# A fused attention, gate and projection kernel: a new written-out table of order, engines and PSUM banks

## The chip, the cores and the metric

The kernel runs on one core of one Trainium2 chip. The metric is device time in microseconds (us): the time of one execution of the whole program, the median of three runs. A profile comes from one further execution, whose own time is given beside it.

## The reference, cut to what matters

There are 8 batches of 8 heads, 576 positions and 64 columns a head. Per head, attention with a cumulative decay:

```
scores = scale * q @ k.T
cum    = cumsum(log(clip(f, 1e-4, 1)))
scores = where(causal, -1e9, scores + cum[:, None] - cum[None, :])
attn   = exp(scores - max);  attn = attn / (sum(attn) + 1e-9)
x      = attn @ v                      # heads side by side: 512 columns
gate   = sigmoid(conv1d over 5 positions of x, one filter a column)
out    = (gate * (x @ w_val)) @ w_out  # both 512 x 512
```

## The kernel before, in words

The work is cut into 32 pairs of heads (four pairs make a batch) and, after every fourth pair, into the two projections of a batch. Every piece of work is a node of a `Plan`: it has a class, the engines that may run it, what it reads and writes, and the PSUM banks that it needs. The classes of one pair, in the order in which they depend on each other:

- loads by DMA, all issued from SyncE: `Xr` (q and k of the pair, two buffers), `vt` (v, two buffers), `dm` (the decay table of one head, broadcast to 128 rows, three buffers) and `dl` (its last part, two halves, two buffers). `dm` and `dl` come from the DRAM table `decd`, which the kernel writes at its start (`tabD`, two transfers; pairs 8 and later read the second).
- `sel`: GpSimd masks `dm` (L314); GpSimd or VectorE adds `tri` to `dl` (L317).
- `TH`, `TL` (from pair 4 on): `Xr` is split into a high part `Xh` (L268) and a low part `Xl` (L394).
- `S` on TensorE in three parts (u = 0, 1, 2; L253), into PSUM; `red` on VectorE (L462) adds the decay and takes the row minimum into `negm`; `SX` on ScalarE (L466) is the exponential into `P` or `Pl`, with its row sum; `rec` (L475, L476) on VectorE takes the reciprocal `rz`.
- `norm`: P times `rz`, on ScalarE (L273), VectorE or GpSimd (L275).
- `PT`: transposes of P on TensorE (L507; L525 and L526 for `Pl`); `PE`: their copies from PSUM to `pt`, on ScalarE or VectorE (L268).
- `PV` on TensorE in two parts (L253), `X`: the copy to `x` (L268), `xh` and `xl`: its high and low part (L268, L576), `conv`: five steps on the gate (the first on any engine, L273 or L275; four on VectorE, L609), `sig`: tanh (L583). For the first two pairs the convolution is a matmul (`CV`) instead.
- per batch `Mv` (x @ w_val, 16 banks of two parts, L253), `H` (times the gate, L641), `hh` and `hl` (high and low, L268, L655), `Mo` (@ w_out, L253), `O` (the copy out, L682 or L684) and `OD` (its DMA).

At the start the two weights come in as 64-bit numbers and are taken apart by VectorE and ScalarE (classes `wv`, `wo`; L698 to L735), in the same first 60 us or so in which the first pairs run. Six blocks of transposes of the identity (`warm`, L368) keep TensorE at work there.

No scheduler runs in the kernel. The order, the engine of each node and its PSUM banks are read from a string, `TABLE`:

```
n, e = DIGITS.index(table[at]) * 64 + DIGITS.index(table[at + 1]), ENGINES[int(table[at + 2])]
...
for k in nd["take"]:
    self.home[k] = range(int(table[at]), int(table[at]) + self.width[k])
    at += 1
...
yield nd["fn"], e
```

Three characters name a node and its engine, and one more each bank that it is the first to touch. Nodes are emitted in the order of the table, so each engine, SyncE's DMA queue among them, runs its own nodes in that order and waits at the first that is not ready. The durations and `mode` numbers that `pe`, `load` and the others are given (`1.55`, `cols=`, `mode=`) were used to find the table; the emitted program does not depend on them.

Of the kernel before, what the change touches and what calls it, by code (L numbers as in the profile page):

```python
# [41 lines left out]
002d001232e02l20W10y32j22o0452m12h23a40X30o40_22x062f20A32k12i12r22t20w30-
12c32g12s10t001122n23c42B31212E11742Q002p22q12v22w13e44n42K012u12y24t43g44r42z12C32D23i41021323m32M022N12O032P22R21422L12A24l41512G12I11621i43z0453p02
3673I005x41a22F33E21912H13u23v13q22S060x33A23n33r12T13s23t12U023C22V13w22J33G22W0633532_021c23x12-
12X12Z11b21d13y23D13o22Y231033J23K13N33B14T061e21g21f23214z25F43P13015D41h21t41k11l23H13F14x34U23_004011n21m23L21o136014V13U2450023311p23Q23711q21r24p
44714A0345649163014613R14v45z41s21E43M24F24811v15L31y23V001w26423T13X073S34G143054B21z13W16514y38T441001x23Y14C11A24413O21B27D48V45J31C14D24H24K0127F4
7x44214E14P24R24L21D31H23Z034I14J23-138054a008_24Z24X34M14N24Y31G14Q14S14O14c014b14g21J21K14-
24W250152156005714d158023911I25914_254035517M15B45e041L25a005b15121M25321O25K35c015g0255d21P45W0365h15j15k21N15f27L36125X25M001275Z25i27N34e14f27z4343
7O15R24j045Y16215_21R15-17J36015T25S15P25N25U11S25O15Q11U26626f16b11V18N48P47P24h031T24i187065n006c25V27B45l016914k16811-
# [759 lines left out]
```

## Time and profile before

| | |
|---|---|
| median of 3 runs | 541.58 us (541.3 to 542.08) |
| the profiled execution | 540.74 us, span 539.0 us |
| granted TensorE clock | 0.999 of full speed |
| busy: TensorE matmul, VectorE, ScalarE, GpSimd | 515.9, 468.1, 424.5, 241.9 us |
| DMA | 95.44 MB, 52.5% of 16 engines |

The span goes from the first to the last instruction; 1.7 us of the profiled execution lie outside it. PE is TensorE's matmuls, PEld its weight loads, DVE is VectorE, ACT ScalarE, POOL GpSimd, SP SyncE. The end of a matmul is modelled in the profile, so a busy PE can hide a short wait.

### The profile page before, as it was taken

What the parts mean: (1) busy time and instruction counts of PE and PEld (TensorE: products, weight loads), DVE (VectorE), ACT (ScalarE), POOL (GpSimd) and SP (SyncE); (2) the same over time, 40 slices, a digit from 0 to 9 for tenths busy, and PEclk for the clock granted to TensorE, in tenths of its full rate; (3) what the DMA queues carried; (4) which work ended last, traced back from release to release, by engine and by line L of the source; (5) the groups of instructions that cost most, each with busy time, mean ns of one, the idle gap of its engine ahead of it and who ended that gap; (6) DMA issues with size and microseconds to landing.
All of it is one profiled execution on the core that took longest, in us unless ns stands there. A gap on an engine that the chain in (4) does not pass through costs nothing.

```text
span 539.0 us, 12792 instructions
## 1 busy us (share of the span) xinstructions
PE 515.9 (96%) x4412; PEld 448.6 (83%) x4412; DVE 468.1 (87%) x1288; ACT 424.5 (79%) x1160; POOL 241.9 (45%) x338
## 2 busy tenths in 40 slices
PE   7878999999999999999999999999999999999997
PEld 5556778888888888888889888899898987898995
DVE  7979999899998998989899989988989897877850
ACT  5989999998678788769987989998888867664312
POOL 3523458363443645365525736657353725123210
PEclk9999999999999999999999999999999999999999
DMA  7987685464446558256575547565475432510112
GB/s 264 280 301 244 210 283 175 143 195 175 162 140 202 176 178 277 93 175 231 181 227 179 161 172 245 196 215 201 165 246 169 150 125 105 198 65 1 40 39 99
DMA packets 29905, 95.44 MB, mean 177 GB/s; under 512 B 3920, under 2 KB 3920, under 8 KB 29840
## 3 DMA queue, kind: packets, MB, share of 16 engines
q1 hardware_dynamic: 29840, 94.62, 52.5%
q8 instruction: 35, 0.57, 0.4%
q14 instruction: 30, 0.25, 0.2%
HBM read 84.69 MB, written 9.91 MB: 176 GB/s over the span
## 4 chain that ended last, share of the span: by engine, by line
PE 61%; DVE 19%; ACT 8%; DMA 5%; issue 4%; SPq 1%; POOL 0%; DVEq 0%; ACTq 0%; POOLq 0%
PE banks L253 51%; PE banks L507 8%; DVE banks L462 5%; DVE gate L609 4%; DMA dl<-decd 3%; ACT P L466 3%; PE banks L525 2%; DVE pt L268 1%; DMA out_dram<-ot 1%; ACT pt L268 1%; SPq L280 1%; DVE P L275 1%; DVE Xl L394 1%; DMA Xr<-in_x_dram 1%; DVE negm L462 1%
## 5 line engine op out<-in xcount | busy, mean ns | idle before, releaser
L466 ACT ACTIVATE P<-banks,negm 128x384 f32<-128x384 f32 (+3 forms) x256 | 135.3, 544 | 25.6 <-DVE negm L462 22.4
L462 DVE CUSTOM_DVE_ANT_0 banks<-banks,dm 128x512 f32<-128x512 f32 (+3 forms) x256 | 119.6, 516 | 9.4 <-PE banks L253 4.0
L253 PE MATMUL banks<-xh,wall 128*128 128x288 f32 x512 | 119.0, 305 | 1.5 <-ACT P L466 0.7
L609 DVE SCALAR_TENSOR_TENSOR gate<-x,cw,gate 128x576 f32<-128x576 f32 x120 | 109.0, 913 | 1.2
L268 ACT COPY pt<-banks 128x256 f32<-128x256 f32 (+2 forms) x217 | 90.3, 451 | 21.7 <-PE banks L507 14.6
L253 PE MATMUL banks<-pt,vt 128*64 128x128 f32 (+2 forms) x1408 | 95.7, 290 | 3.9 <-DVE pt L268 3.0
L314 POOL TENSOR_SCALAR_AFFINE_SELECT dm<-dm 128x256 f32<-128x256 f32 x126 | 62.3, 520 | 80.6 <-DMA dm<-decd 57.6
L507 PE MATMUL banks<-ident,P 128*128 128x128 f32 x640 | 93.1, 276 | 4.9 <-ACT P L466 1.7
L253 PEld LDWEIGHTS banks<-pt,vt 128*64 128x64 f32 x1408 | 83.9, 137 | 15.1 <-issue 5.7
L253 PE MATMUL banks<-wall,hh 128*128 128x512 f32 x288 | 93.3, 405 | 1.2 <-ACT P L466 1.2
L253 PEld LDWEIGHTS banks<-xh,wall 128*128 128x128 f32 x512 | 86.1, 188 | 4.8 <-ACT P L466 1.4
L507 PEld LDWEIGHTS banks<-ident,P 128*128 128x128 f32 x640 | 72.8, 140 | 17.1 <-ACT pt L268 2.7
L275 POOL TENSOR_SCALAR P<-P,rz 128x512 f32<-128x512 f32 (+3 forms) x67 | 48.2, 725 | 72.8 <-DVE rz L476 45.1
L253 PE MATMUL banks<-xl,wall 128*128 128x288 f32 x256 | 75.4, 295 | 0.0
L273 ACT ACTIVATE P<-P,rz 128x512 f32<-128x512 f32 (+3 forms) x117 | 65.6, 586 | 3.8 <-DVE rz L476 3.4
L253 PEld LDWEIGHTS banks<-wall,hh 128*128 128x128 f32 x288 | 50.2, 188 | 10.3 <-ACT P L466 1.7
L253 PE MATMUL banks<-Xh 128*128 128x288 f32 (+4 forms) x280 | 57.2, 338 | 1.3 <-DVE h L641 0.6
L253 PE MATMUL banks<-wall,hl 128*128 128x512 f32 x144 | 56.6, 393 | 0.0
L466 ACT ACTIVATION_READ_ACCUMULATOR P<-banks,negm 128x1 f32 x256 | 55.9, 218 | 0.0
L253 PE MATMUL banks<-Xl,Xh 128*128 128x288 f32 (+4 forms) x280 | 53.1, 313 | 0.1
L253 PE MATMUL banks<-Xh,Xl 128*128 128x288 f32 (+4 forms) x280 | 53.1, 313 | 0.0
L253 PEld LDWEIGHTS banks<-xl,wall 128*128 128x128 f32 x256 | 48.2, 188 | 0.2
(109 smaller groups left out, 871.9 us busy)
## 6 DMA issues: line engine op xcount, KB each, us to landing
dm<-decd SPq DMA_DIRECT2D x62, 640.0 KB, 5.2
Xr<-in_x_dram SPq DMA_DIRECT2D x32, 608.0 KB, 5.5
vt<-in_v_dram SPq DMA_DIRECT2D x32, 320.0 KB, 4.5
out_dram<-ot SPq DMA_DIRECT2D x36, 256.0 KB, 3.7
dl<-decd SPq DMA_DIRECT2D x62, 144.0 KB, 4.5
ot<-in_w_val_dram SPq DMA_DIRECT2D x2, 512.0 KB, 5.3
wu<-in_w_val_dram SPq DMA_DIRECT2D x2, 512.0 KB, 8.9
ot<-in_w_out_dram SPq DMA_DIRECT2D x2, 512.0 KB, 5.8
```

The costliest lines, as they stand in the source:

```text
L253: nc.tensor.matmul(out, lhsT=lhsT, rhs=rhs, start=start, stop=stop)
L268: (eng.copy if eng is nc.scalar else eng.tensor_copy)(out=out, in_=in_)
L273: eng.activation(out=out, in_=in_, func=AF.Copy, scale=col)
L275: eng.tensor_scalar(out=out, in0=in_, scalar1=col, scalar2=0.0, op0=ALU.mult, op1=ALU.add)
L280: lambda e: (nc.sync if e == "SP" else nc.scalar).dma_start(out=out, in_=in_), reads, writes, **kw)
L314: nc.gpsimd.affine_select(out=t, in_=t, pattern=[[0, 2], [-1, P]], base=0, channel_multiplier=1, compare_op=ALU.is_ge, fill=-BIG)
L394: eng.tensor_tensor(out=Xl[r][:, a:e], in0=Xr[r][:, a:e], in1=Xh[r][:, a:e].bitcast(F32), op=ALU.subtract)
L462: nc.vector.tensor_tensor_reduce(out=sl, in0=sl, in1=add[:, o:o + ext], op0=ALU.add, op1=ALU.min, scale=-0.125, scalar=3.0e38, accum_out=n ...
L466: nc.scalar.activation(out=dst[:, o:o + ext], in_=bank(key)[:, c0:c0 + ext], func=AF.Exp, bias=negm[r][:, col], scale=-1.0, accum_out=zs[r ...
L507: nc.tensor.transpose(out=bank(key)[:, c:c + P], in_=Pt[m][:, BOFF[b] + P * j:BOFF[b] + P * j + P], identity=ident)
L525: nc.tensor.transpose(out=bank(key)[:, P * j:P * j + P], in_=Pl[r][:, D + P * j:D + P * j + P], identity=ident)
L609: eng.scalar_tensor_tensor(out=gt, in0=src, scalar=wt_, in1=gt, op0=ALU.mult, op1=ALU.add)
```

## The change

The table is another one for the same 2868 entries: all lines of it differ. Every node has the same function, reads and writes, and every matmul, transfer and copy is still there once. What differs is the order on each engine, the banks, and, for classes that more than one engine may run, which engine it is. Counted in the two tables (where the counts differ by more than 2):

| class | before | after |
|---|---|---|
| `norm` on ScalarE, VectorE, GpSimd | 137, 75, 76 | 113, 49, 126 |
| `TH` on ScalarE, VectorE, GpSimd | 24, 14, 18 | 28, 3, 25 |
| `TL` on VectorE, GpSimd | 29, 27 | 25, 31 |
| `PE` copies on ScalarE, VectorE | 217, 103 | 206, 114 |
| `X` on ScalarE, VectorE | 46, 18 | 51, 13 |
| `xh` on ScalarE, VectorE | 23, 9 | 19, 13 |
| `hh` on ScalarE, VectorE | 22, 10 | 17, 15 |
| `hl` on VectorE, GpSimd | 21, 11 | 18, 14 |
| `O` on ScalarE, VectorE | 23, 13 | 27, 9 |
| `sel` on GpSimd, VectorE | 83, 12 | 88, 7 |

The first transfers of SyncE's queue are, before: f, f, conv_w, w_val, vt(1), Xr(0), w_val, vt(0), decd(0), Xr(1), decd(1), dm(2), w_val, dm(0), dm(1), dl(0), dl(1), dl(0), dl(1), Xr(0), w_val, Xr(1). After: f, f, conv_w, w_val, w_val, Xr(0), vt(1), vt(0), decd(0), Xr(1), dl(1), dl(1), dm(2), w_val, dm(0), dl(0), dl(0), Xr(0), dm(1), w_val, dl(1), Xr(1), decd(1).

The other edits change numbers that only served to find the table:

```diff
-0240630040B30930C40E10b20430u000r010N40s000a20c20d10520F20H20I10G20z30e20J20f23k40q010h10K20g20740Y40L20k10l12940i20j20M20P10m42b30Q20S20T10R20U20V20v
...
+0040b20x30930240C40a20E10430520c20y30F20s010H20G20d10e20630t000I10J20f20N40K20Y40g20L20j20M20k20l20740h10i10P10Q20S20R20T10u000U20W10r003k42940m43a42d
...
-        load("load", 1.55, i - (1.0 if i else 9.0), Xr[r], x[i], (), [("Xr", r)], early=i == 0)
+        load("load", 1.95, i - (1.0 if i else 9.0), Xr[r], x[i], (), [("Xr", r)], early=i == 0)
...
-            load("dec", 1.6, p + 0.05 * h, dm[m], decd[2 * i + h:2 * i + h + 1, 0:SW].to_broadcast([P, SW]), dk, [("dm", m)])
+            load("dec", 2.05, p + 0.05 * h, dm[m], decd[2 * i + h:2 * i + h + 1, 0:SW].to_broadcast([P, SW]), dk, [("dm", m)])
...
-        load("tabD", (0.7, 2.0)[n], z - 0.5, decd[r0:r1], st[r0:r1], [*ktab, *kst], [("decd", n)])
+        load("tabD", (0.35, 0.9)[n], z - 0.5, decd[r0:r1], st[r0:r1], [*ktab, *kst], [("decd", n)])
...
-            pe("S", (1.15, 0.905, 0.87)[u] * more * two, p, go, opd + tab,
+            pe("S", ((1.15, 0.902, 0.79), (1.41, 0.97, 1.067))[i < NF][u] * two, p, go, opd + tab,
...
-            pe("PT", 0.109 * nt, p, go, [("ident",), *(("P", m, b) for b in blocks)], [key], cols=256 * nt, mode=0)
+            pe("PT", 0.109 * nt, p, go, [("ident",), *(("P", m, b) for b in blocks)], [key], cols=256 * nt, mode=2)
...
-            load(nm + "D", 1.8, p - 0.5, wu[w], src[c * P:(c + 1) * P].bitcast(I32), (), uk + kl)
+            load(nm + "D", 1.3, p - 0.5, wu[w], src[c * P:(c + 1) * P].bitcast(I32), (), uk + kl)
```

## Rows read from the trace of the kernel before

**Rows 1.** The page: busy time, share of the span and instructions of each engine; then the engines' shares of the chain of work that ended last.

```profile
PE 515.9 (96%) x4412; PEld 448.6 (83%) x4412; DVE 468.1 (87%) x1288; ACT 424.5 (79%) x1160; POOL 241.9 (45%) x338
PE 61%; DVE 19%; ACT 8%; DMA 5%; issue 4%; SPq 1%; POOL 0%; DVEq 0%; ACTq 0%; POOLq 0%
```

**Rows 2.** Busy time of each engine in five stretches: the stretch, its length, then PE, PEld, DVE, ACT and POOL busy us (with instruction counts), the granted clock, the DMA share and GB/s.

```profile
0.00:31.00 31.00, 22.68 (x153) 16.42 (x153) 24.09 (x79) 21.59 (x57) 13.39 (x36) 1.00 0.89 275
31.00:141.00 110.00, 104.04 (x894) 85.76 (x891) 104.32 (x296) 101.26 (x276) 51.88 (x66) 1.00 0.63 211
141.00:475.00 334.00, 328.91 (x2946) 292.38 (x2946) 303.82 (x843) 278.17 (x774) 164.16 (x224) 1.00 0.54 181
475.00:535.00 60.00, 60.00 (x430) 54.04 (x426) 35.90 (x73) 22.89 (x54) 12.48 (x13) 1.00 0.13 46
535.00:539.03 4.03, 0.25 (x2) 0.00 (x0) 0.00 (x0) 0.60 (x1) 0.00 (x0) 0.81 0.35 130
```

**Rows 3.** The timeline at the start: start us, duration us, engine, line, operation, tiles and shapes, count, and in brackets the idle time before it with what ended it.

```profile
3.00 4.53 PE L368 MATMUL banks<-ident 128*128 128x128 f32 x20 [3.00 <-POOL ident L323]
10.23 1.56 PE L253 MATMUL banks<-Xr 64*128 64x512 f32 x8 [0.48 <-DMA Xr<-in_x_dram]
29.07 0.23 DVE L317 TENSOR_TENSOR dl<-dl,tri 128x64 f32<-128x64 f32 x1 [2.75 <-DMA dl<-decd]
29.57 1.64 PE L253 MATMUL banks<-pt,vt 128*64 128x192 f32 x20 [2.63 <-DVE pt L268]
```

**Rows 4.** The chain of work that ended last, in order of time: start us, us, what.

```profile
3.63 6.56 DMA Xr<-in_x_dram
19.30 9.68 DMA dl<-decd
```

**Rows 5.** SyncE's queue at the start: when a transfer was issued, and for how long the queue was at it.

```profile
3.63 0.43 SPq L280 DMA_DIRECT2D Xr<-in_x_dram  x1
12.66 0.33 SPq L280 DMA_DIRECT2D dm<-decd  x1
17.52 2.37 SPq L280 DMA_DIRECT2D dl<-decd  x4
```

**Rows 6.** Transfers in the first 40 us: all of them, then by destination and source the count, KB each and the median us from issue to landing.

```profile
DMA packets 3363, 11.22 MB, mean 281 GB/s; under 512 B 573, under 2 KB 573, under 8 KB 3360
dm<-decd SPq DMA_DIRECT2D x5, 640.0 KB, 7.0
Xr<-in_x_dram SPq DMA_DIRECT2D x4, 608.0 KB, 8.4
wu<-in_w_val_dram SPq DMA_DIRECT2D x2, 512.0 KB, 8.9
vt<-in_v_dram SPq DMA_DIRECT2D x3, 320.0 KB, 6.2
dl<-decd SPq DMA_DIRECT2D x6, 144.0 KB, 8.8
```

**Rows 7.** Groups of instructions by line, engine, operation and shape: count, busy us and mean ns of one, then the idle time before them and what ended it.

```profile
L609 DVE SCALAR_TENSOR_TENSOR gate<-x,cw,gate 128x576 f32<-128x576 f32 x120 | 109.0, 913 | 1.2
L275 POOL TENSOR_SCALAR P<-P,rz 128x512 f32<-128x512 f32 x20 | 16.8, 845 | 19.8 <-DVE rz L476 13.4 <-ACT pt L268 3.6 <-PE banks L253 1.4
L273 ACT ACTIVATE P<-P,rz 128x512 f32<-128x512 f32 x30 | 21.9, 738 | 0.6 <-DVE rz L476 0.5
L275 DVE TENSOR_SCALAR P<-P,rz 128x512 f32<-128x512 f32 x14 | 7.1, 508 | 0.2
L268 POOL CAST Xh<-Xr 128x576 fp32r<-128x576 f32 x12 | 8.2, 686 | 4.9 <-DMA Xr<-in_x_dram 4.9
L268 DVE CAST Xh<-Xr 128x576 fp32r<-128x576 f32 x6 | 3.6, 608 | 0.0
```

**Rows 8.** Single lines: count, then ns of one, shortest/median/longest, first and last start us, shapes.

```profile
L609 DVE SCALAR_TENSOR_TENSOR gate<-x,cw,gate x120: 778/819/1993, 68.3 to 511.1; 128x576 f32<-128x576 f32 x120
L314 POOL TENSOR_SCALAR_AFFINE_SELECT dm<-dm x126: 398/407/1098, 3.2 to 469.9; 128x256 f32<-128x256 f32 x126
L275 DVE TENSOR_SCALAR P<-P,rz x72: 259/410/1581, 17.3 to 474.8; 128x256 f32<-128x256 f32 x22, 128x384 f32<-128x384 f32 x19, 128x128 f32<-128x128 f32 x17, 128x512 f32<-128x512 f32 x14
L275 POOL TENSOR_SCALAR P<-P,rz x67: 364/692/1602, 16.2 to 487.7; 128x512 f32<-128x512 f32 x20, 128x128 f32<-128x128 f32 x20, 128x256 f32<-128x256 f32 x16, 128x384 f32<-128x384 f32 x11
```

**Rows 9.** TensorE alone, around a change from transposes to `PV` and from `PV` to `Mv`, and inside a run of `Mv`.

```profile
502.12 0.38 PE L507 MATMUL banks<-ident,P 128*128 128x128 f32 x2
502.43 2.95 PE L253 MATMUL banks<-pt,vt 128*64 128x192 f32 x44
505.31 0.40 PE L253 MATMUL banks<-xh,wall 128*128 128x288 f32 x1
505.55 0.30 PE L253 MATMUL banks<-xl,wall 128*128 128x288 f32 x1
...
512.95 0.30 PE L253 MATMUL banks<-xh,wall 128*128 128x288 f32 x1
513.08 0.29 PE L253 MATMUL banks<-xl,wall 128*128 128x288 f32 x1
```

**Rows 10.** Who waited for whom, in total: us, times, longest.

```profile
POOL P L275 <- DVE rz L476: 45.1, 16, 6.0
ACT P L466 <- DVE negm L462: 22.4, 25, 2.6
```

More of the change, by code (lines that the diff above doesn't have):

```diff
@@ L40 @@
 TABLE = """
-0240630040B30930C40E10b20430u000r010N40s000a20c20d10520F20H20I10G20z30e20J20f23k40q010h10K20g20740Y40L20k10l12940i20j20M20P10m42b30Q20S20T10R20U20V20v
[L42 to L49, printed above, removed]
@@ new lines @@
+37437607a2aX1e21c407dD3g24dT0542729V1c517728F2dJ02613262br47b1bW2dC3dU2eI4283d-
+2c22c01b707dQ2dR19X1dK2b503dL1fW4dW28G3c31ce02dM2fY4dO2dP17c37e0dY2dZ1bY3b62c12dN1c603b81b_37i06cc079Y2eK49Z2b91dS2bb17f19W27g47j0eW2c71d_1e52cf1cd17n
+019-
+2ha4dX19_2ba2e41e72cg074cj2eU37o0ch2dV17k1ca00ck1e32e93eb3bc2ci28M1fg02fh2bd2gb1cb1be2fi1ef05hi4e62cn07eS37p1g91cl03e81eZ02401cm17q4dA4eT3co2cp2f7063c
+r3eg1ea3e-
+2f22hg4f31e_1gc3ed05f02f42fe2f11fa2ho3a017s07eh00f51ee2ei1cq37l47t07u1el02cA04fb1ec2ej01cB0hr1ek1f82ff1g63cs2cx05cy0bf2f62em1bg1ep023cC2ct2er1cI04fm1f
@@ L370, in tile_decay_attention_gated_mlp @@
         wk = new(("warm", n))
-        pe("warm", 0.436, z, lambda wk=wk: warm(wk), [("ident",)], [wk], cols=1024, mode=0)
+        pe("warm", 0.436, z, lambda wk=wk: warm(wk), [("ident",)], [wk], cols=1024, mode=2)
     def mk_tri():
@@ L526, in gol @@
             nc.tensor.transpose(out=bank(key4)[0:D, 0:P], in_=Pl[r][:, 0:D], identity=ident)
-        pe("PT", 0.48, p, gol, [("ident",), ("Pl", r)], [key, key4], cols=1152, mode=0)
+        pe("PT", 0.545, p, gol, [("ident",), ("Pl", r)], [key, key4], cols=1152, mode=2)
         for h in range(2):
@@ L564, in plan_pv @@
             names = ((1, 2), (3, "l", "l4"))[half]
-            pe("PV", (1.36, 1.515)[half], p, go, [*vk, *(("pt", m, n) for m in ms for n in names), *(("pt0", m) for m in ms)], [key],
+            pe("PV", (1.36, 1.465)[half], p, go, [*vk, *(("pt", m, n) for m in ms for n in names), *(("pt0", m) for m in ms)], [key],
                cols=(6144, 7168)[half], mode=3)
@@ L599, in gocv @@
                         mm(bank(key)[:, 0:e - a], dv[t], xr[:, t + a:t + e], t == 0, t == KC - 1)
-                pe("CV", 2.55, p + 0.1 + 0.02 * half, gocv, [*xk, ("xpad", r), *dk], [key], cols=5760, mode=0)
+                pe("CV", 2.55, p + 0.1 + 0.02 * half, gocv, [*xk, ("xpad", r), *dk], [key], cols=5760, mode=2)
                 act("CE", 0.3, p + 0.1 + 0.02 * half, lambda key=key, a=a, e=e: half_tanh(gt[:, a:e], bank(key)[:, 0:e - a]), [key], [gk])
@@ L636, in plan_moe @@
                     cs = (2 * c2, 2 * c2 + 1)
-                    pe("Mv", 0.8, p + 0.5 * MS * c2, go, [*((x, (G * b + c) % NX) for c in cs for x in ("xh", "xl")),
+                    pe("Mv", 0.79, p + 0.5 * MS * c2, go, [*((x, (G * b + c) % NX) for c in cs for x in ("xh", "xl")),
                                                          *((w, c) for c in cs for w in ("wv", "wvh"))], [key], cols=1728, mode=0)
@@ L674, in plan_moe @@
                 js2 = (2 * half, 2 * half + 1)
-                pe("Mo", 1.37, p + half * MS, go, [*((x, jj, n) for jj in js2 for x in ("hh", "hl") for n in names),
+                pe("Mo", 1.36, p + half * MS, go, [*((x, jj, n) for jj in js2 for x in ("hh", "hl") for n in names),
                                                  *((w, jj) for jj in js2 for w in ("wo", "woh"))], [key], cols=3072, mode=0)
```

137 lines of the change are left out of this document (71 added, 66 removed).

## The prediction

> **What bounds the kernel now.** I began with the page. TensorE's matmuls are busy for 515.9 of 539.0 us and hold 61% of the chain that ended last; VectorE follows with 468.1 us and 19% [rows 1]. The number and the shapes of the matmuls are the same in both tables, so the order can only give back time in which TensorE waits, or what it loses when it changes from one form of matmul to another. Its visible idle time is 23.1 us, and the table of stretches says where it lies [rows 2]: 31.0 - 22.7 = 8.3 us up to 31 us, 110.0 - 104.0 = 6.0 us from 31 to 141 us, 334.0 - 328.9 = 5.1 us from 141 to 475 us, nothing from there to 535 us, and 3.8 us at the end. The granted clock is 1.00 in the four stretches that hold matmul work, so no clock is to be won. The last 3.8 us are the last copy and its transfer, which both tables order alike. Of the first 8.3 us, 3.0 are the wait for the identity, also left as it is [rows 3]. So 8.3 - 3.0 + 6.0 + 5.1 = 16.4 us can be won in what the profile shows. It is a floor: ends of matmuls are modelled, and a short wait disappears in them.
>
> The three stretches have different causes. At the start the largest single wait of TensorE is 2.63 us, before the second half of the first `PV`, for a small VectorE copy [rows 3]. That copy stood behind VectorE's `dl` add, which had waited 2.75 us for a transfer [rows 3]; that transfer was issued at 19.30 us and took 9.68 us [rows 4]. From 31 to 141 us VectorE is busy for 104.3 of 110 us (95%) and ScalarE for 101.3 (92%) [rows 2]: here these two set the pace, since the weights are decoded beside the pairs. From 141 to 475 us they fall to 91% and 83% [rows 2]; what TensorE waits for then is short and comes from single chains.
>
> **The change, part by part.**
>
> *Transfers at the start.* The late `dl` is moved ahead of the second `decd` table, three `dm`, one `w_val` block and the two `dl` of the other buffer. By the sizes [rows 6] that is at least 3 x 640 + 512 + 2 x 144 = 2720 KB, which at the 281 GB/s of the first 40 us [rows 6] is 9.7 us. In the old queue the first `dm` went out at 12.66 us, and the four `dl` began at 17.52 us [rows 5]. The add on `dl(1)` is GpSimd's in the new table, so that VectorE would not stand before it even if it were late. I count the 2.6 us as gone. Against it, `Xr(0)` now has a second `w_val` (512 KB) ahead of it instead of a `vt` (320 KB): 192 KB or 0.7 us later. It was issued at 3.63 us and took 6.56 us [rows 4, 5], and TensorE waited 0.48 us for it [rows 3], so nothing covers the delay at that point. Net 2.6 - 0.7 = 1.9 us. The bounds are 0 (VectorE, freed, runs into the extra decoding below) and 2.6.
>
> *Work moved between engines.* I priced each node by the time from its start to the start of its engine's next node, the lower quartile of its class and size, which leaves queueing and collisions out; the groups of rows show the order of size. A normalisation of 128x512 takes 508 ns on VectorE, 738 on ScalarE and 845 on GpSimd; a cast `TH` of 128x576 takes 608 on VectorE and 686 on GpSimd [rows 7]. By these sums VectorE's work falls from 424 to 412 us, ScalarE's from 399 to 382, and GpSimd's rises from 208 to 251. Where it falls matters more. Along the first 120 us of matmul work, which end at 141 us in the old run, VectorE goes from 121.4 to 114.8 us, ScalarE from 115.5 to 114.6, GpSimd from 55.4 to 75.2. Within it, the first 60 us get 2.5 us heavier on VectorE (61.6 to 64.1) and stay level on ScalarE (59.0 and 59.1); from 60 to 120 VectorE loses 9.1 us (59.8 to 50.7). VectorE is therefore no longer saturated in the second half; in the first it has more to do, which the 2.75 us of waiting removed above pays for. Of the 6.0 us I count 2.5 as won: not all, because ScalarE hardly gets lighter there. Bounds: 0 and 6.0.
>
> *Chains in the middle.* For each of the 595 steps of TensorE I took the latest matmul step on which it depends through other engines, added the row durations of the nodes between, and compared that with the matmul work that the table puts between the two. This says nothing of queues; it counts places where the order leaves little room. Steps with less than 1 us of room fall from 103 to 62: from 14 to 14 in the first 60 us of matmul work, 13 to 10 in the next 60, 66 to 34 from 120 to 440, 10 to 4 behind that. Where the number is halved I take half of the visible 5.1 us, 2.5 us. Bounds: 0, since the new order has places of its own (a `vt` issued 2.2 us of matmul work ahead of its `PV`, where a `vt` of the first 40 us took 6.2 us to land [rows 6]), and 5.1.
>
> *Changes of form.* Three forms follow each other on TensorE: full tiles (`Mv`, `Mo`, `PT`, `S` u = 2), 64 rows (`S` u = 0, 1) and 64 columns (`PV`). After a `PV` the first `Mv` matmul takes 0.24 us to the next start, 505.31 to 505.55, where inside a run it takes 0.13, 512.95 to 513.08 [rows 9]: about 0.1 us a change. The tables have 130 and 127 changes: 0.3 us. Bounds 0.3 and, were every change 0.2 us, 0.6. The Trainium skill (TensorEngine Tiling (Array Packing), Key Properties) says that a change of tiling mode drains TensorE. The rows agree that a change costs something; with three fewer of them the sum stays as it is.
>
> *Nothing else in the diff reaches the chip:* the other numbers were only used to search.
>
> Sum: 1.9 + 2.5 + 2.5 + 0.3 = 7.2 us off the profiled 540.7 us: 533.5 us. The median of the runs lies 0.8 us above the profiled execution, so a median of 533.5 to 534.3; I say 534, and 0.2% (1.1 us) is about what a measurement of this kernel can tell from no change.
>
> **The rivals.**
>
> *The waits form again.* A table fixes who waits for whom; a wait that goes may only move. For it speaks that ScalarE is at 92% from 31 to 141 us and keeps its 114.6 us there, and that VectorE has 2.5 us more in the first 60. If the middle gains nothing and the saturated stretch 0.5, the sum is 1.9 + 0.5 + 0.3 = 2.7 us: 538 to 539 us. Against it: room grew in the middle in nearly half of the tight places.
>
> *GpSimd and VectorE hold each other up; the kernel gets slower.* The trace shows that they do: the convolution steps (L609) take 778 ns at best, 819 in the median, 1993 at worst, with a mean of 913 [rows 7, 8], which is 120 x 0.094 = 11.3 us lost by VectorE on this line alone, and GpSimd's masks go from 398 to 1098 ns [rows 8]. The new table gives GpSimd some 70 more instructions, 50 of them normalisations between `rec` and a transpose, where GpSimd already is idle for 45.1 us before `rz` is there [rows 10] and so starts at once, colliding with whatever VectorE does next. If each held VectorE up for half of a 0.6 us instruction, that is 70 x 0.3 = 21 us against the 12 us taken off it: 9 us more, of which the stretch up to 141 us, which gets 19.8 of the 43 us, has 4. With the 1.9 us of the start that makes 544 us; with late transposes in the middle as well, 548. It decides from about 12 / 0.3 = 40 collisions of 70 on. Against it: at the present rate, 11.3 us for 241.9 us of GpSimd, 43 us more cost L609 2 us. The Trainium skill (SBUF — State Buffer, Who interferes with whom) states the rule behind this: GpSimd and a VectorE instruction with two SBUF inputs, or in a two-port mode, exclude each other for a whole instruction. The spread of L609 agrees; by that rule a normalisation moved to GpSimd saves VectorE less than its length.
>
> *More than the sum.* If both saturated engines let go from 31 to 141 us and the waits hidden in modelled ends go as well, 1.9 + 6.0 + 5.1 + 0.3 = 13.3 us: 527 to 528 us.
>
> *The change does nothing,* because what differs is hidden: excluded by the 2.6 us wait, unless something equal takes its place; that is the first rival at its far end.
>
> **How the numbers follow.** Forecast (530 to 537 us) 0.55; waits form again (537 to 541.5) 0.20, of which 0.06 within 0.2%; slower 0.13, nearly all of it above 543; more than the sum (under 530) 0.10; 0.02 for what I don't see, put at no change. Faster 0.55 + 0.10 + 0.14 = 0.79, within 0.2% 0.08, slower 0.13. The range leaves out the slow case and the far end of the best: 527.5 to 541.5; the forecast's own is 530 to 537.
>
> **What would show it.** Right: no wait of over 1 us before a `PV` in the first 35 us, and no VectorE `dl` add behind a transfer; TensorE's first `S` some 0.7 us later; VectorE under 90% busy in the second half of the stretch up to 141 us, PE idle there about 3.5 us; in the middle about 2.5 us; GpSimd about 290 us busy, L609's mean still near 0.9 us. Wrong: L609's mean above 1.05 us, or transposes (L507) that wait for GpSimd's P; or the 2.6 us found again under another name before 60 us.

## The result, and the profile after

The new table runs in 526.69 us, the median of four runs (525.57 to 527.36); the old one beside it in 541.44 us (538.9 to 542.08). The ratio is 0.9734, with an interval of 0.9698 to 0.977: 14.8 us less. Beside the later runs the old kernel took 539.7 to 540.5 us in the median, so 13 to 15 us is what the change is worth. The forecast was 534.0 us, with a range of 527.5 to 541.5: the direction was right, the gain about twice as large, and the time lies 0.8 us outside the range. The profiled execution took 527.36 us, its span 525.6 us (539.0 before). Line numbers of the new kernel are 3 higher than those of the old (L609 is now L612, L507 is L510, L253 is L256).

The page of the new kernel: busy time, then the engines' shares of the chain that ended last. It answers [rows 1].

```profile
PE 510.6 (97%) x4412; PEld 448.0 (85%) x4412; DVE 450.2 (86%) x1257; ACT 410.1 (78%) x1121; POOL 292.1 (56%) x408
PE 79%; ACT 9%; DVE 5%; DMA 3%; issue 2%; SPq 1%; POOL 0%; DVEq 0%; ACTq 0%
```

VectorE's share of the chain fell from 19% to 5%, TensorE's rose from 61% to 79%. And TensorE is busy for 5.3 us less than before, with the same 4412 matmuls at the same granted clock. Since the ends of matmuls are modelled, that can hardly be quicker arithmetic. It is mostly waiting that the old profile showed as work, as the count from start to start below bears out.

Stretches of the new run; it answers [rows 2] (columns as there), with the second stretch in two halves.

```profile
0.00:31.00 31.00, 24.73 (x162) 17.70 (x163) 25.81 (x82) 22.78 (x59) 14.84 (x40) 1.00 0.80 265
31.00:86.00 55.00, 51.45 (x429) 40.34 (x429) 51.81 (x151) 53.27 (x149) 37.35 (x50) 1.00 0.73 242
86.00:141.00 55.00, 54.36 (x492) 48.92 (x489) 49.67 (x140) 49.67 (x135) 36.01 (x49) 1.00 0.58 192
141.00:475.00 334.00, 333.12 (x3020) 300.16 (x3019) 294.30 (x832) 270.47 (x755) 196.90 (x267) 1.00 0.55 182
521.00:525.60 4.60, 0.89 (x4) 0.38 (x3) 0.00 (x0) 0.60 (x1) 0.00 (x0) 1.00 0.29 110
```

The same two halves of the old run:

```profile
31.00:86.00 55.00, 50.42 (x403) 38.77 (x400) 51.97 (x156) 54.59 (x153) 24.35 (x31) 1.00 0.70 234
86.00:141.00 55.00, 53.62 (x493) 46.98 (x492) 52.34 (x141) 46.67 (x124) 27.53 (x35) 1.00 0.56 189
```

Visible idle time of TensorE is now 6.3 us up to 31 us (8.3 before), 3.6 + 0.6 = 4.2 us up to 141 us (6.0), 0.9 us up to 475 us (5.1) and 3.7 us at the end (3.8): 8.1 us less in all, of 13.4 us by which the span fell. The rest is in the counts. From 141 to 475 us the old run issued 2946 matmuls [rows 2], the new one 3020 in the same 334 us. A busy matmul took 328.91 / 2946 = 111.6 ns there, now 333.12 / 3020 = 110.3 ns. The mix of shapes in the two windows is not quite the same, but 1.3 ns x 3020 = 4 us is most of the 5.3 us that the busy time lost.

The start of the new run (timeline; columns as in [rows 3]):

```profile
10.48 2.07 PE L256 MATMUL banks<-Xr 64*128 64x512 f32 x8
17.59 0.44 PE L510 MATMUL banks<-ident,P 128*128 128x128 f32 x2 [1.17 <-ACT P L276]
26.02 2.94 PE L256 MATMUL banks<-pt,vt 128*64 128x128 f32 x44
```

The whole first `PV` follows without a wait, where 2.63 us stood before its second half [rows 3]. Groups by shape, against [rows 7], and the single line of the convolution, against [rows 8]:

```profile
L612 DVE SCALAR_TENSOR_TENSOR gate<-x,cw,gate 128x576 f32<-128x576 f32 x120 | 104.9, 879 | 1.3
L278 POOL TENSOR_SCALAR P<-P,rz 128x512 f32<-128x512 f32 x27 | 22.1, 819 | 31.8 <-DVE rz L479 23.7 <-ACT gate L586 6.1 <-DVE rz L478 2.1
```

```profile
L612 DVE SCALAR_TENSOR_TENSOR gate<-x,cw,gate x120: 778/819/1744, 67.8 to 503.3; 128x576 f32<-128x576 f32 x120
```

With 50 us more on GpSimd the mean of the convolution step fell from 913 to 879 ns, the longest from 1993 to 1744. So the extra work on GpSimd did not lengthen this step in the new order.

**Waits counted from start to start.** Busy time hides waits, starts don't. For each of TensorE's 595 steps I took the time from its last matmul's start to that of the next step, and, as the time that this transition needs, about the quickest sixth of the same pair of kinds in the old run. The sum of the latter is called matmul work (500.6 us before, 499.1 after); what is above it is waiting: 30.5 us before, 19.0 after. With the first matmul at 2.7 instead of 3.0 us this makes 1.5 + 11.5 + 0.3 = 13.3 of the span's 13.4 us. By place, on the scale of matmul work: up to 25 us 7.7 and 6.6; from 25 to 120 us (141 us of time in the old run) 10.8 and 8.4; from 120 to 440 us 11.5 and 3.7; behind that 0.5 and 0.4. So the middle gave 7.8 us, three times the term in the forecast. The split depends on how the pairs are grouped: grouped by class of step alone, the same starts give 30.9 us before and 18.2 after, 14.6 and 8.5 of them in the middle. Other groupings put the fall in the middle between 6 and 9 us, more than twice the term in each.

### The profile page after: what moved, and what is told of

Its sections match the earlier page's. It is cut to its first block, busy times and chain, and to the rows that moved or that the text cites. A ratio compares the mean times of both kernels' runs of the same rounds, so it can differ in the third digit from the quotient of the medians.

```text
span 525.6 us, 12791 instructions
## 1 busy us (share of the span) xinstructions
PE 510.6 (97%) x4412; PEld 448.0 (85%) x4412; DVE 450.2 (86%) x1257; ACT 410.1 (78%) x1121; POOL 292.1 (56%) x408
## 4 chain that ended last, share of the span: by engine, by line
PE 79%; ACT 9%; DVE 5%; DMA 3%; issue 2%; SPq 1%; POOL 0%; DVEq 0%; ACTq 0%
PE banks L256 64%; PE banks L510 12%; ACT P L469 3%; PE banks L528 2%; DMA Xr<-in_x_dram 2%; DVE banks L465 2%; ACT P L276 1%; ACT pt L271 1%; DMA dm<-decd 1%; SPq L283 1%; DMA Pl<-in_f_dram 1%; PE banks L529 1%; ACT Xh L271 0%; ACT gate L701 0%; ACT x L271 0%
## 5 line engine op out<-in xcount | busy, mean ns | idle before, releaser
L469 ACT ACTIVATE P<-banks,negm 128x128 f32<-128x128 f32 (+3 forms) x256 | 134.2, 535 | 22.0 <-DVE negm L465 20.7
L278 POOL TENSOR_SCALAR P<-P,rz 128x128 f32<-128x128 f32 (+3 forms) x113 | 77.4, 691 | 98.0 <-DVE rz L479 69.4
L465 DVE CUSTOM_DVE_ANT_0 banks<-banks,dm 128x128 f32<-128x128 f32 (+3 forms) x256 | 120.0, 513 | 11.5 <-PE banks L256 4.5
L256 PE MATMUL banks<-xh,wall 128*128 128x288 f32 x512 | 120.2, 306 | 0.0
L612 DVE SCALAR_TENSOR_TENSOR gate<-x,cw,gate 128x576 f32<-128x576 f32 x120 | 104.9, 879 | 1.3
L510 PE MATMUL banks<-ident,P 128*128 128x128 f32 x640 | 99.2, 276 | 4.2 <-ACT P L276 1.2
L271 ACT COPY pt<-banks 128x512 f32<-128x512 f32 (+2 forms) x206 | 84.5, 444 | 22.4 <-PE banks L510 10.7
L256 PE MATMUL banks<-pt,vt 128*64 128x128 f32 (+2 forms) x1408 | 95.6, 290 | 0.3 <-DVE pt L271 0.3
L256 PE MATMUL banks<-wall,hh 128*128 128x512 f32 x288 | 93.3, 405 | 0.0
L256 PEld LDWEIGHTS banks<-pt,vt 128*64 128x64 f32 x1408 | 83.6, 137 | 11.2 <-issue 2.4
L510 PEld LDWEIGHTS banks<-ident,P 128*128 128x128 f32 x640 | 75.4, 140 | 16.5 <-POOL P L278 1.8
L256 PEld LDWEIGHTS banks<-xh,wall 128*128 128x128 f32 x512 | 86.3, 188 | 0.7
L256 PE MATMUL banks<-xl,wall 128*128 128x288 f32 x256 | 75.4, 294 | 0.0
L317 POOL TENSOR_SCALAR_AFFINE_SELECT dm<-dm 128x256 f32<-128x256 f32 x126 | 56.7, 475 | 29.4 <-DMA dm<-decd 21.8
L271 DVE COPY pt<-banks 128x512 f32<-128x512 f32 (+2 forms) x114 | 49.3, 450 | 17.1 <-PE banks L510 10.4
L276 ACT ACTIVATE P<-P,rz 128x256 f32<-128x256 f32 (+3 forms) x100 | 58.2, 597 | 5.9 <-DVE rz L479 5.8
L256 PE MATMUL banks<-Xh 128*128 128x288 f32 (+4 forms) x280 | 57.6, 340 | 0.4 <-ACT P L469 0.4
L256 PEld LDWEIGHTS banks<-wall,hh 128*128 128x128 f32 x288 | 50.2, 189 | 7.7 <-ACT P L469 0.2
L256 PE MATMUL banks<-wall,hl 128*128 128x512 f32 x144 | 56.7, 394 | 0.0
L256 PE MATMUL banks<-Xh,Xl 128*128 128x288 f32 (+4 forms) x280 | 52.9, 313 | 0.0
L256 PE MATMUL banks<-Xl,Xh 128*128 128x288 f32 (+4 forms) x280 | 52.9, 313 | 0.0
```

Source lines behind the costliest of these rows:

```text
L256: nc.tensor.matmul(out, lhsT=lhsT, rhs=rhs, start=start, stop=stop)
L271: (eng.copy if eng is nc.scalar else eng.tensor_copy)(out=out, in_=in_)
L276: eng.activation(out=out, in_=in_, func=AF.Copy, scale=col)
L278: eng.tensor_scalar(out=out, in0=in_, scalar1=col, scalar2=0.0, op0=ALU.mult, op1=ALU.add)
L317: nc.gpsimd.affine_select(out=t, in_=t, pattern=[[0, 2], [-1, P]], base=0, channel_multiplier=1, compare_op=ALU.is_ge, fill=-BIG)
L465: nc.vector.tensor_tensor_reduce(out=sl, in0=sl, in1=add[:, o:o + ext], op0=ALU.add, op1=ALU.min, scale=-0.125, scalar=3.0e38, accum_out=n ...
```

## Experiments

Theory: the new order is fitted to its engines, so that TensorE finds its data in the middle; each stretch earns its part by itself. Rivals: it is less load on VectorE and ScalarE that does it, or the new engines by themselves, or the quicker start. One thing is not separated: the PSUM banks and SyncE's queue went with the order in every run but two on the queue's start, so "order" below means all three together. In kernels with a spliced or exchanged table the lines have other numbers again (L242 is L253, L496 is L507, L306 is L317, L598 is L609 of the old kernel; L610 is L609 where work is cut). All runs in one table, waits by place in matmul work:

| kernel | median us | up to 21.5 | 21.5 to 134.5 | 134.5 to 275 | behind | sum |
|---|---|---|---|---|---|---|
| before | 541.44 | 7.6 | 11.3 | 6.0 | 5.7 | 30.5 |
| after | 526.69 | 6.4 | 8.6 | 1.1 | 2.9 | 19.0 |
| ordB_engA | 599.37 | 6.3 | 20.3 | 30.0 | 31.7 | 88.4 |
| ordA_engB | 595.20 | 8.9 | 23.3 | 25.2 | 30.5 | 87.9 |
| b_norm_A | 552.04 | 6.3 | 12.4 | 12.2 | 12.0 | 42.9 |
| a_norm_B | 563.96 | 10.1 | 19.5 | 7.5 | 17.4 | 54.5 |
| b_dve_short | 533.80 | 5.6 | 10.7 | 3.7 | 3.0 | 22.9 |
| b_act_short | 538.19 | 5.7 | 11.2 | 6.4 | 5.9 | 29.2 |
| b_pool_short | 538.04 | 4.6 | 11.8 | 4.9 | 6.5 | 27.7 |
| b_all_short | 528.85 | 5.0 | 7.3 | 2.4 | 2.7 | 17.5 |
| a_dve_short | 525.22 | 5.7 | 7.2 | 1.4 | 2.1 | 16.4 |
| a_all_short | 522.41 | 5.2 | 5.3 | 1.1 | 2.5 | 14.1 |
| b_dl_early | 539.64 | 5.5 | 11.5 | 6.0 | 6.5 | 29.5 |
| a_xr_first | 526.04 | 5.2 | 8.2 | 1.2 | 3.7 | 18.3 |
| ab_177 | 539.48 | 6.0 | 12.9 | 6.6 | 6.4 | 32.0 |
| ba_177 | 528.20 | 6.8 | 6.5 | 1.1 | 2.8 | 17.2 |
| ab_892 | 536.16 | 6.2 | 10.5 | 6.2 | 6.2 | 29.1 |
| ba_892 | 534.56 | 5.9 | 13.4 | 3.4 | 3.4 | 26.1 |
| ab_1716 | 529.82 | 6.6 | 8.4 | 1.2 | 6.3 | 22.5 |
| ba_1716 | 538.95 | 5.2 | 12.6 | 7.0 | 3.3 | 28.0 |

The old kernel beside these runs took 539.7 to 540.5 us in the median; where a few tenths matter the ratio is given. A row is one profile: before and ba_1716 have the same table up to 275 us of matmul work and yet read 7.6 and 5.2, 11.3 and 12.6, 6.0 and 7.0 us there, so a difference of 1 or 2 us between two cells tells nothing.

### Order or engines

One kernel keeps the old order and banks and takes the new engine of every node, the other does the reverse; 484 of 1036 nodes that have a choice change engine. The edit of the string is written out here in words:

```diff
 entry of the old table, in the old order:
-(node, engine_before[node], banks_before[node])
+(node, engine_after[node], banks_before[node])
 and in the new order:
-(node, engine_after[node], banks_after[node])
+(node, engine_before[node], banks_after[node])
```

> The order and the banks of the kernel before, with every node on the engine that the new table gives it. Theory 1 (the order on TensorE gives the time, by the room that it leaves between dependent steps): this kernel has 111 matmul steps with less than 1 us of room, as the one before (103), so it stays at 539 to 545 us, or gets slower by what badly placed nodes cost. Theory 2 (the relief of VectorE and ScalarE gives the time): VectorE is 12 us and ScalarE 17 us lighter here too, so most of the 14.8 us comes: 528 to 533 us.

> The order and the banks of the new table, with every node on the engine that it had before. Theory 1 (order and room): 63 steps with less than 1 us of room, as the new kernel (62), so most of the gain stays: 527 to 532 us. Theory 2 (relief of VectorE and ScalarE): the load is the old one, 536 to 542 us. Sum of the two: if each gives a part, both crossed kernels lie between 529 and 539 us.

Measured: 599.37 us, ratio 1.1098 (1.1056 to 1.1139), and 595.20 us, 1.1017 (1.0972 to 1.1061). Both theories fell: neither part alone gains anything, each costs: 59 us against the old kernel, 68 us against the new one. In the first, transposes wait for everybody; the second line is the old kernel's:

```profile
L496 PE MATMUL banks<-ident,P 128*128 128x128 f32 x640 | 96.8, 279 | 23.6 <-DVE pt L257 5.8 <-ACT P L455 4.9 <-POOL P L264 4.8
L507 PE MATMUL banks<-ident,P 128*128 128x128 f32 x640 | 93.1, 276 | 4.9 <-ACT P L466 1.7 <-ACT P L273 1.1 <-DVE P L275 0.9
```

23.6 us of idle time stand before this line instead of 4.9. The second also has 63 places with less than 1 us of room by my count, as few as the new kernel (62), and 87.9 us of waits: the count that carried the forecast's middle term does not predict waits once queues are disturbed. An engine runs its nodes in the table's order, so a node on another engine delays all that stands behind it there. Not all of the 87.9 us is waiting for data: in the second kernel the granted clock is 0.97 from 141 to 475 us, where both originals have 1.00, and by that figure some 0.03 x 334 = 10 us (an estimate) are lost to the lower clock:

```profile
141.00:475.00 334.00, 302.63 (x2567) 262.45 (x2565) 275.33 (x735) 247.77 (x680) 153.37 (x206) 0.97 0.49 163
```

The milder exchange, of the 288 normalisations alone (171 change engine):

```diff
 normalisations in the old order:
-(node, engine_before[node], banks_before[node])
+(node, engine_after[node], banks_before[node])
 normalisations in the new order:
-(node, engine_after[node], banks_after[node])
+(node, engine_before[node], banks_after[node])
```

> The old order and banks; only the 288 normalisations run on the engines of the new table (171 change engine, 50 more on GpSimd), all else on the old engines. Theory 1 (only together): in proportion to the full exchange, 58 us for 484 nodes, 20 us: 555 to 565 us. Theory 2 (the normalisations on GpSimd are the gain): 528 to 535 us. Theory 3 (hardly matters): 539 to 543 us. The forecast's slower rival (GpSimd holds VectorE up, 544 to 548 us) would show here as a mean of L609 above 1.05 us.

> The new order and banks; only the 288 normalisations run on the engines that the old table gave them (171 of them change engine, GpSimd goes from 126 back to 76), all else on the new engines. Theory 1 (order and engines of a table only work together, every node on another engine stands in a queue that was not laid out for it): in proportion to the full exchange, 70 us for 484 nodes, 171 nodes cost 25 us: 545 to 556 us. Theory 2 (the normalisations on GpSimd are what the change gains by): their gain alone is lost, some 540 us. Theory 3 (where a normalisation runs hardly matters): 527 to 530 us.

Measured: 552.04 us, ratio 1.0227 (1.0206 to 1.0247), and 563.96 us, 1.0448 (1.0418 to 1.0478). The costs are 12 us and 37 us where proportion gave 20 and 25. Both times lie outside every range that was expected: only together, yes, in proportion, no. The new order depends on where its normalisations run three times as much as the old. The first run also tests the slower rival of the forecast: 50 more normalisations on GpSimd, in an order that was not made for them. The kernel does get slower, but not by a longer convolution step. Its line, that of b_pool_short (next section; GpSimd's normalisations and masks cut), and the transposes of the first run:

```profile
L598 DVE SCALAR_TENSOR_TENSOR gate<-x,cw,gate 128x576 f32<-128x576 f32 x120 | 107.7, 902 | 1.5 <-ACT gate L262 0.3
L610 DVE SCALAR_TENSOR_TENSOR gate<-x,cw,gate 128x576 f32<-128x576 f32 x120 | 102.3, 857 | 1.2
L496 PE MATMUL banks<-ident,P 128*128 128x128 f32 x640 | 95.3, 279 | 12.8 <-DVE P L264 3.7 <-ACT P L455 2.4 <-POOL P L264 2.0
```

The mean is 902 ns against 913 in the old kernel. What grew is the idle time before the transposes, from 4.9 to 12.8 us, waiting for P from all three engines; the kernel lost 12 us. By these rows it is late data in the queues that costs, not two engines that hold each other up. The Trainium skill (SBUF — State Buffer, Who interferes with whom) lets such pairs exclude each other. The spread of single instructions agrees [rows 8], and b_pool_short shows a price: with less work on GpSimd the step takes 857 ns, 6.7 us less on this line than in the old kernel. That more work on GpSimd lengthens the step, no run here shows.

### Load or order

Work of one engine is cut while order and engines stay: convolution steps on 64 of 576 columns and VectorE's normalisations on 16 (VectorE), normalisations on 16 columns (ScalarE), normalisations and masks on 16 (GpSimd), and the three together. The edit for VectorE:

```diff
-                times(eng, sl, sl, rz[r][:, c:c + 1])
+                w = 16 if eng in (nc.vector,) else sl.shape[-1]
+                times(eng, sl[:, 0:w], sl[:, 0:w], rz[r][:, c:c + 1])
...
-                    eng.scalar_tensor_tensor(out=gt, in0=src, scalar=wt_, in1=gt, op0=ALU.mult, op1=ALU.add)
+                    eng.scalar_tensor_tensor(out=gt[:, 0:64], in0=src[:, 0:64], scalar=wt_, in1=gt[:, 0:64], op0=ALU.mult, op1=ALU.add)
```

> The kernel before, with VectorE's work cut: its 120 convolution steps (L609) work on 64 of 576 columns and its normalisations on 16, which takes some 90 us off VectorE and nearly all of its collisions with GpSimd on these lines; the output leaves that work out. If VectorE's pace, its own load and what GpSimd takes from it, is what makes TensorE wait in the old order, most of the 14.8 us comes: 526 to 530 us. If the old order itself leaves too little room, or the other engines are late, it stays above 535 us.

> The kernel before, with ScalarE's 137 normalisations cut to 16 columns, some 45 us off ScalarE; the output leaves that work out. If ScalarE's pace makes TensorE wait (92% busy up to 141 us, 83% behind that): 528 to 534 us. If not: 538 to 541 us.

> The kernel before, with GpSimd's normalisations and masks cut to 16 columns, some 80 us of its 242; the output leaves that work out. If late GpSimd results and its collisions with VectorE are what the old table did not foresee and the new one does: 528 to 534 us. If neither matters: 538 to 541 us.

> The kernel before, with the three cuts together. This is the floor of the old order on TensorE: matmul work, changes of form, transfers and chains that no relief shortens. If the pace of the engines is the whole difference to the new kernel: at or under 526 us. If the old order on TensorE is itself worse: 530 us or more.

Measured in the old order: VectorE 533.80 us, 0.9873 (0.9832 to 0.9914); ScalarE 538.19, 0.9952 (0.9931 to 0.9973); GpSimd 538.04, 0.9951 (0.9928 to 0.9975); all three 528.85, 0.9793 (0.9752 to 0.9833). The first and the last lie between the ranges that were expected. Of the three cuts VectorE's takes most: behind 134.5 us of matmul work 5.0 of 11.7 us of waits. Up to there it takes hardly any, though VectorE falls from 104.3 to 93.8 us of work between 31 and 141 us; TensorE issues as many matmuls in that stretch as in the old kernel, 894 [rows 2]:

```profile
31.00:141.00 110.00, 104.15 (x894) 86.14 (x894) 93.77 (x300) 101.23 (x277) 49.55 (x68) 1.00 0.62 209
```

With all three cut the old order still takes 528.85 us, more than the new order with its full work, 526.69. In the middle the cuts leave VectorE 249 us and ScalarE 254 us of work, where the new table leaves them 294 and 270. So less load alone is not what the change gained by; that it has a part in the gain is not excluded.

> The new table, with VectorE's work cut: the convolution steps (L612) on 64 of 576 columns and VectorE's normalisations on 16 columns, the same cut that took the old table from 540.5 to 533.8 us. Only the amount of work is changed, so the output is not the reference's. Theory 1 (the new order has taken out what TensorE waited for VectorE in the middle, 12.3 us down to 3.7): little is left to take, 1.5 to 3 us, so 523.5 to 525.5 us, with 2.5 us or more of waiting left between 120 and 440 us of matmul work. Theory 2 (VectorE sets the pace of the new table as well, the gain came from somewhere else): as much is taken as from the old one, 6.7 us or more, so 520 us or less.

> The new table, with the work of VectorE, ScalarE and GpSimd cut together as in the old table's run at 528.85 us (convolution steps on 64 columns, normalisations and masks on 16); the output is not the reference's. Theory 1 (the gain of the change lies in an order that fits its engines, so that load matters less in it): the cut takes less than the 12 us that it took from the old table, 4 to 7 us: 520 to 523 us. Theory 2 (the two orders differ only in how much work they put beside TensorE): with the work gone both come out alike, 527 to 529 us, or the cut takes as much as before, 12 us, 515 us.

Measured in the new order: 525.22 us, 0.9726 (0.9706 to 0.9746), and 522.41 us, 0.9671 (0.9651 to 0.9692). The VectorE cut, worth 6.2 us to the old order, is worth 1.5 us here at most (by the ratios, 0.9726 against 0.9734, less than half of that); all three, worth 11.2 us, give 4.3 us. Both times lie in the first theory's ranges. The middle shows it by the count of matmuls in one stretch; before and after have 2946 and 3020 there.

The old order, VectorE cut:

```profile
141.00:475.00 334.00, 332.10 (x2997) 298.52 (x2996) 255.61 (x851) 280.00 (x785) 150.00 (x224) 1.00 0.55 183
```

The old order, all three cut:

```profile
141.00:475.00 334.00, 332.58 (x3008) 299.41 (x3007) 249.02 (x841) 254.20 (x785) 122.72 (x226) 1.00 0.54 181
```

The new order, all three cut:

```profile
141.00:475.00 334.00, 333.23 (x3023) 300.03 (x3023) 243.10 (x825) 248.64 (x751) 135.07 (x268) 1.00 0.56 181
```

The new order with its full work issues 3020 matmuls, with the three cuts 3023: in its middle the work that was cut costs TensorE next to nothing. It is not all of the work, for VectorE and ScalarE are still busy for 243 and 249 of the 334 us. The old order gets from 2946 to 3008 with the same cuts and stays 12 short of the new order with its full work.

### Each stretch by itself

Up to some entries the two tables name nearly the same nodes (3 of 177, 7 of 892 and 5 of 1716 differ). There they can be spliced (the splices at 1716 in the same way).

```diff
-TABLE = before
+TABLE = after[:892] + [e for e in before if e.node not in after[:892]]
 and its mirror image:
-TABLE = after
+TABLE = before[:892] + [e for e in after if e.node not in before[:892]]
```

> New table up to its 892nd entry (134 us of matmul work, some 155 us of time), then the old table's order, engines and banks for all that is left; the first 892 entries of the two tables name the same nodes but for 7. From the starts of the matmuls, the new run reaches this seam 4.6 us ahead of the old one (153.4 against 158.0 us). Theory 1 (each stretch of the new order carries its own part of the gain): the old order behind the seam keeps its own waits, 540.4 - 4.6 = 536 us, 534.5 to 537.5, and the two kernels spliced at this entry add up to the two originals, 540.4 + 526.7 = 1067 us, within 3 us. Theory 2 (a table only works as a whole: what goes before sets how late the queues run in what follows): 3 us or more worse than that, 539 us or more, or all of the gain is here, 530 us or less.

> The mirror image: the old table up to its 892nd entry, then the new table's order, engines and banks for the rest. Theory 1 (each stretch carries its own part): 13.4 - 4.6 = 8.8 us off the old time, 531.6 us, 530 to 533.5. Theory 2 (the middle of the new order is only quick because its start was): 535 us or more.

> New table up to its 1716th entry (275 us of matmul work, some 300 us of time; 5 of 1716 nodes differ), then the old one. By the starts of the matmuls the new run is 9.5 us ahead there (294.7 against 304.2 us). Theory 1 (own part in each stretch): 540.4 - 9.5 = 530.9 us, 529 to 533. Theory 2 (only as a whole): 534 us or more, or the full gain, 527.5 us or less.

> The old table up to its 1716th entry, then the new one. Theory 1 (own part in each stretch): 13.4 - 9.5 = 3.9 us off, 536.5 us, 534.5 to 538. Theory 2: 539.5 us or more, so that the later part gains nothing by itself.

Measured: ab_892 536.16 us, 0.9925 (0.9906 to 0.9944), where 536 was expected; ab_1716 529.82, 0.981 (0.9793 to 0.9828), where 530.9 was; ba_892 534.56, 0.9903 (0.9864 to 0.9941), 3 us more than expected; ba_1716 538.95, 0.9984 (0.9954 to 1.0014), 2.4 us more and between the two theories, with ten runs from 536.1 to 542.8. Of the four, ab_892 and ab_1716 lie in the first theory's ranges, the two others in none. The waits show where: behind the seam ab_892 has 6.2 and 6.2 us, the old order's 6.0 and 5.7; ab_1716 has 8.4 and 1.2 before its seam (the new order's 8.6 and 1.1) and 6.3 behind; ba_1716 has 3.3 behind its seam (the new order's 2.9). ba_892 has 3.4 and 3.4 where the new order has 1.1 and 2.9, and 13.4 in front instead of 11.3. That is the seam: a wait of 1.93 us for a normalisation at 157.6 us, and then a stretch at a lower clock (last section). The pairs of mirror images add up to 1070.7 and 1068.8 us against 1066.4 for the originals (539.7 + 526.7); the first pair misses the 3 us that were allowed by 0.7, and the seam's wait and clock are of that size. So the stretches up to both seams earn their part by themselves, and ba_892, 5.1 us under the old kernel in spite of its seam, shows the same for what lies behind 892. For the last stretch it isn't shown by the time: ba_1716 is 0.7 us under the old kernel, an interval that takes in no change, and only its waits behind the seam, 3.3 against 5.7 us, speak for it.

### The start

The old table with the two late `dl` moved up, the new table with `Xr(0)` ahead of the second `w_val`, and the splice at entry 177:

```diff
 SyncE's queue of the old table:
-decd(0), Xr(1), decd(1), dm(2), w_val, dm(0), dm(1), dl(0), dl(1), dl(0), dl(1), Xr(0), w_val, Xr(1)
+decd(0), Xr(1), dl(1), dl(1), dm(2), w_val, dm(0), dm(1), dl(0), dl(0), Xr(0), w_val, Xr(1), decd(1)
 of the new table:
-conv_w, w_val, w_val, Xr(0), vt(1)
+conv_w, w_val, Xr(0), w_val, vt(1)
 and the splice:
-TABLE = before
+TABLE = after[:177] + [e for e in before if e.node not in after[:177]]
```

> The kernel before, with three entries of SyncE's queue moved at the start: both dl(1) transfers right behind Xr(1), the second decd table behind the second Xr(1). All else as before. If the 2.6 us wait before the second half of the first PV is time of the whole kernel: 539 to 539.5 us, and no wait of over 1 us before that PV. If VectorE and ScalarE, which are over 90% busy up to 141 us, set the pace there, the wait comes back as others before 141 us, and the time is within 0.2% of before: 540.5 to 542.5 us.

> The new kernel, with one entry of SyncE's queue moved: Xr(0) ahead of the second w_val block instead of behind it (512 KB). If the first S stands on the path, it starts about 1 us earlier and the kernel ends 0.5 to 1.5 us earlier: 525 to 526 us. If what follows is bound by VectorE and ScalarE, the start moves and the end doesn't: 526.2 to 527.2 us.

> New table up to its 177th entry (21 us of matmul work, some 34 us of time; 3 of 177 nodes differ), then the old one. Here the new run is 1.7 us ahead of the old one (33.3 against 35.0 us), most of it the late dl of the old queue. Theory 1 (each stretch carries its own part): 1.7 us off, some 538 us. Theory 2 (what the start gains is given back in the stretch up to 141 us, as when the dl alone was moved): no gain, 539 to 540 us.

> The old table up to its 177th entry, then the new one. Theory 1 (own part in each stretch): 13.4 - 1.7 = 11.7 us off, some 528 us. Theory 2 (the start's gain is given back at once whichever order follows): the late dl costs nothing in the end either, 527 us or less, as quick as the whole new table. Theory 3 (the stretch up to 141 us is only quick behind the new start): 531 us or more.

Measured: b_dl_early 539.64 us, 0.9984 (0.9964 to 1.0005); a_xr_first 526.04, 0.9737 (0.9702 to 0.9772), 0.65 us under the new kernel, too little to tell from it; ab_177 539.48, 0.9982 (0.9962 to 1.0002); ba_177 528.20, 0.9765 (0.9724 to 0.9806). By the medians the start is worth 0.8 to 1.5 us, at the edge of what the runs can tell: ab_177 came out by the second theory's number, ba_177 by the first's, and the intervals of b_dl_early and ab_177 take in no change. b_dl_early and a_xr_first lie between the two ranges expected of them. In b_dl_early the wait before the second half of the `PV` is gone:

```profile
26.00 2.96 PE L242 MATMUL banks<-pt,vt 128*64 128x128 f32 x44 [0.18 <-ACT pt L257]
```

Against the old profile ab_177 is 2.5 us ahead at 21.5 us of matmul work (32.5 us) and 0.9 us at 134.5 (157.1 us). Most of the 2.5 us is that the old profile was late there, as the spliced runs show. ba_892, ba_1716 and ba_177 have the old start unchanged, and so the same late `dl`; in two of them, ba_892 and ba_1716, the same two lines stand so (timeline):

```profile
27.43 0.23 DVE L306 TENSOR_TENSOR dl<-dl,tri 128x64 f32<-128x64 f32 x1 [1.59 <-DMA dl<-decd]
27.92 1.64 PE L242 MATMUL banks<-pt,vt 128*64 128x192 f32 x20 [1.38 <-DVE pt L257]
```

```profile
26.71 0.23 DVE L306 TENSOR_TENSOR dl<-dl,tri 128x64 f32<-128x64 f32 x1 [0.75 <-DMA dl<-decd]
27.20 1.64 PE L242 MATMUL banks<-pt,vt 128*64 128x192 f32 x20 [0.54 <-DVE pt L257]
```

The wait of 2.63 us [rows 3] was that of one execution, in which the transfer took 9.68 us [rows 4]; here it is 1.38 and 0.54 us, in ba_177 0.53. By the starts of the matmuls the four profiles with the old start reach 21.5 us of matmul work at 35.0, 33.3, 32.6 and 32.2 us, those with the new start at 33.3 (after), 33.1, 33.5 and 32.5 us: means of 33.3 and 33.1. By these profiles the new start gains next to nothing, though two of those four (after and ab_1716) met slow matmuls at 8 us, as told in the next section.

## Why the forecast was off, step by step

**The start (1.9 us forecast).** The mechanism is there: `dl` late, VectorE behind it, `PV` behind VectorE. The profiled pair shows 1.1 us of waits and 0.3 us of an earlier first matmul. But the 2.6 us was the long end of a spread, as the old start's other profiles show (0.5 to 1.4 us), so the term should have been under 1 us. The first `S` came 0.25 us later (10.23 to 10.48 us), not 0.7; the identity was ready 0.3 us earlier. Contrary to the forecast, TensorE did not wait for `Xr` there: it was busy with the eight matmuls ahead, which took 2.93 us in the new run and 1.56 us in a_xr_first:

```profile
7.76 2.93 PE L256 MATMUL banks<-gate,dm 64*128 64x512 f32 x8 [1.41 <-DVE gate L361]
7.79 1.56 PE L242 MATMUL banks<-gate,dm 64*128 64x512 f32 x8 [1.69 <-DVE gate L347]
```

That is about half the pace, and the forecast had no term for it. Whether the granted clock was the lower one isn't shown: the new run's trace has no record of it before 11.7 us. As forecast, no VectorE `dl` add of the new run waits for a transfer.

**Up to 141 us (2.5 us).** The number is right, 2.4 us by starts and 1.8 us visible (4.2 us of idle time left, where the forecast had 3.5), but the mechanism isn't shown, so this is in part luck. The forecast let the gain come from VectorE's relief in the second half. VectorE did go from 52.34 to 49.67 of 55 us there, 95% to 90%, at the bound that I had named; but 1.0 of the 1.8 us was gained in the first half, where VectorE stayed at 52 us. And b_dve_short, with VectorE at 93.8 instead of 104.3 us in the stretch, takes only 0.6 us of the waits from 21.5 to 134.5 us; ScalarE's cut takes 0.1 us, GpSimd's none, all three together 4.0 us. So VectorE alone doesn't set the pace there. 3.6 of the 4.2 us that are left visible stand in the first half, where ScalarE is still at 53.27 of 55 us.

**The middle (2.5 us).** This is the step that failed, by its size: 7.8 us where the forecast had 2.5. The direction and the place were right; 0.9 us of idle time are left visible, where the forecast had 2.5. There are two errors in one term, in the same direction. First, the visible 5.1 us were taken for what could be won, although the text called visible idle time a floor; by starts it was 11.5 us. Secondly, "where the number is halved I take half": the waits fell by 7.8 of 11.5 us, two thirds. Half of 11.5 would have made the forecast 530.8 us, and the result would have been inside a range of the same width. The count of places with little room had the right sign and nothing more: ordA_engB has as few of them and waits for 87.9 us. What in the order makes the waits fall, beyond its being fitted to its engines, these runs don't show.

**Changes of form (0.3 us).** The matmul work fell by 1.5 us with three fewer changes (by 0.3 us where the pairs are grouped by class alone). What part of it the changes are, and what part is a short wait that all quick pairs of the old run had as well, these runs don't separate.

**GpSimd.** 292.1 us busy where I had expected about 290, L612's mean 0.88 us where I had said near 0.9. VectorE's busy time fell by 17.9 us, more than the 12 us of the sums; 4.1 us of it are the convolution step, 109.0 to 104.9. The slower rival, as the forecast put it, is out: the step takes no more time in b_norm_A than in the old kernel, and in the new kernel transposes wait for GpSimd's P for 0.7 us in all. "More than the sum", held at 0.10, is what came, though not as put there: the stretch up to 141 us gave 2.4 us, not 6.0, and the waits of the middle that the busy time had hidden gave the rest.

## What to carry to other kernels

An idle time read from a profile with modelled ends is a floor, so take the waits from start to start, or count the matmuls in a stretch, before a term is sized by them. In a kernel whose order is written out, an engine assignment and its order are one thing: a gain can't be put down to the assignment or to relief of an engine unless a run with that alone shows it. A single long wait behind a transfer in one profile is a draw from a spread; look for the same wait in other profiles of the same start before it becomes a term.
